# Moving the preparation of the second layer's weights inside the expert units: earlier start steps, a later low-part step, and four block loads spread over steps

## The chip, the cores and the metric

One core of one Trainium2 chip runs the whole program. The metric is the device time of one execution in microseconds (us); lower is better. The kernel before has a median of 1154.63 us over three runs.

## The reference

Attention in chunks of 32 tokens (batch 4, 8 heads, 768 tokens, 16 tokens of left and 8 of right context, 8 memory slots), then a mixture of 8 experts with the best two per token, then a dense layer of three branches:

```python
scores = scale * np.matmul(q_c, k_full.transpose(0, 1, 3, 2))      # attention, chunk by chunk
out[:, :, c_start:c_end] = np.matmul(softmax(scores), v_full)

h = np.maximum(x[mask] @ w1[e], 0.0)                               # experts: 3072 tokens, 512 -> 1024 -> 512
out[mask] += top2_w[mask, k, None] * (h @ w2[e])

h = np.maximum(np.maximum(x @ w1, x @ w2), x @ w3)                 # dense layer: 512 -> 768 -> 512
return h @ w_out
```

## The kernel before

The program is written out in full, one instruction stream for each engine. The order on an engine is the order in which the Python code emits instructions (a manual schedule); an instruction waits only for the data and the buffers that it needs, and what stands behind it on the same engine waits with it.

**Precision.** Each fp32 matrix product is made of three fp32r products: high part by high part, high by low, low by high (`three`, L274). High parts come from a cast on ACT, low parts from a subtraction on DVE.

**Units.** Each expert is worked off in two units (L283 to L286): an even, long one of 512 token slots (four tiles of 128) and an odd, short one of 320 (tiles of 128, 128 and 64); only expert 0 is cut differently. Unit `u` (L785) first makes `h`: 8 steps (`f` = 0 to 7), each of 12 matmuls into one of two PSUM banks, `sc` and `pp`, emptied by ACT (relu, L807) and DVE (low part, L811). Then it makes `y`: 8 steps for each tile, 3 matmuls each, the result copied out at the eighth (`put`, L664, alternately on ACT and DVE) and written to `ys` in DRAM. So a long unit has steps 0 to 39, a short one 0 to 31, and what the unit does on the side is hung on steps: `side[step]` holds tasks that are emitted behind the matmuls of that step.

**On the side.** (1) The next unit's tokens: `unit_turn(u + 1, j)` turns tile j by four PE transposes, casts it on ACT (L193) and forms its low part on DVE (L194). L819 hangs the four turns of a long unit on steps 12, 20, 28 and 36, ahead of what stands there already. A short unit has three tiles, so within a long unit the last turn that does something is the one at step 28. (2) In long units the next weights of the experts (`plan`, 8 parts at steps 0 to 8). (3) **Pieces** of the second layer's weights, which arrive as 64-bit numbers: 24 pieces of 512 KB, for each of `j` = 9, 10, 11, 0, ..., 8 two halves. `planned` (L158) gives each piece a start step `i` and the steps of its five tasks: `one` (ACT square, DVE L231 and L232), `two` (DVE L235 to L237, then the next load into one of three stage buffers), `three` (DVE L241 and four L246), `four` (ACT cast of the high part into the tile `top`, of which there is one buffer, L251) and `five` (DVE low part L255, then two DMAs on SP's queue to `m2s`, L257). Pieces of `j` = 9 to 11 end within `three`. Short units take one piece at step 9; the long units 2, 6, 10 and 14 (odd expert) take two, the long units 4, 8 and 12 (even expert) three. In units 8 and 12 all three pieces go through all five tasks.

**Block loads.** `quad_load(q)` (L756) reads the finished block q of these weights from `m2s` into the weight slots `room[q]`, 1 MB, by a DMA that POOL issues. `ahead` (L766) calls it for q = 0 to 3 at step 2 of unit 14, the last long one, for 4 and 5 at steps 14 and 20 of unit 15. Blocks 0 to 3 go to slots 4 to 7, which hold the second matrix of expert 6, last read in unit 13. Apart from these, POOL issues the gathers of the next unit's tokens (`fetch`, L262), those of unit 15 at step 0 of unit 14. The dense layer (L1009) follows unit 15.

Of the kernel before, what the change touches and what calls it, by code (L numbers as in the profile page):

```python
# [50 lines left out]
def tile_kernel(ctx, tc, qT, kT, mkT, vw, wgn, noise, w1, w2, m2w, out):  # L51
# [103 lines left out]
    turns = [("f64", j, h) for j in (9, 10, 11, *range(9)) for h in range(2)]  # L155
    wparts, plan = list(range(8)), []

    def planned(u):  # L158

        e = u // 2  # L160
        if u == 0:
            return [(8 + k,) for k in range(4)]
        w = [] if u % 2 else [(8 * e + 4 + k, k, k + 1) for k in range(8) if 8 * e + 4 + k < 8 * E]
        at = [9] if u % 2 else [9, 18, 27] if e % 2 == 0 else [9, 22]
        return w + [(turns.pop(0), i, i + 2, i + 4, i + 5, i + 6) for i in at if turns]

    for u in range(2 * E):
        plan.append(planned(u))
        wparts += [x[0] for x in plan[u]]
# [113 lines left out]
    units = []  # L283
# [467 lines left out]
    def fresh(i):  # L751

        t = (wp if i < 8 else big).tile([128, 2, 1024], F32R, name=f"w{i}")
        return t.rearrange("p r n -> p (r n)")

    def quad_load(q):  # L756

        quads[q] = fresh(room[q]).rearrange("p (o k r n) -> p o k r n", o=4, k=2, r=2)
        POOL.dma_start(quads[q], m2s[q, 4:8].rearrange("o p k r n -> p o k r n"))

    def blocks_of(i):

        for q in i:
            quad_load(q)

    def ahead(u, i):  # L766

        if u == len(units) - 2 and i == 2:
            blocks_of(range(4))
        if u == len(units) - 1 and i in (14, 20):  # L770
            quad_load(4 + (i > 14))
        if u == len(units) - 1:
            for k, task, j in ((AF_[0], block_fetch, 0), (AF_[1], block_fetch, 1), (AF_[2], block_mix, 0), (AF_[3], block_mix, 1),
                               (AF_[4], block_turn, 0), (AF_[4], block_fetch, 2), (AF_[5], block_turn, 1), (AF_[5], block_fetch, 3),
                               (AF_[6], block_mix, 2), (AF_[7], block_turn, 2), (AF_[8], block_mix, 3), (AF_[9], block_turn, 3)):
                if k == i:
                    task(0, j)
# [7 lines left out]
    def unit(u):  # L785
# [11 lines left out]
        for f in range(8):  # L797
            p = psum("p")
            for k in range(4):
                three(p[:, 0:n], parts(wtile(8 * e + k), slice(128 * f, 128 * f + 128)),  # L800
                      parts(xT, k, slice(0, n)), k == 0, k == 3)
                if u == 0 and k < 3:
                    tail(f, k)
            if f == 0 and u:
                unit_fetch(u + 1)
            h = hs[f]
            ACT.activation(h[:, 0, 0:n], p[:, 0:n], AF.Relu)  # L807
            whole = n - ns[-1] % 128
            for o, c in ((h[:, 1], slice(0, whole)), (h[:, 0, n - whole:], slice(whole, n))):
                if c.start < n:  # L810
                    DVE.scalar_tensor_tensor(o[:, c], p[:, c], 0.0, h[:, 0, c].bitcast(F32),  # L811
                                             op0=ALU.max, op1=ALU.subtract)
            for task in side[f]:
                task()
            if u == 0:
                tail(f, 3)
            ahead(u, f)
# [3 lines left out]
        for j, m in enumerate(ns):  # L821
            y = psum("y")
            r0 = CAP * e + 128 * (j0 + j)
            for f in range(8):
                w = parts(wtile(8 * e + 4 + f // 2), slice(512 * (f % 2), 512 * (f % 2) + 512))
                if m == 64:
                    for r in range(2):
                        mm(y, hs[f][:, 0, 128 * j:128 * j + 128], w[r], f + r == 0, f + r == 8)
                else:
                    three(y[0:m], parts(hs[f], slice(128 * j, 128 * j + m)), w, f == 0, f == 7)  # L830
                if f == 7 and m == 64:
                    put_sum(ys[r0:r0 + m, :], y)
                elif f == 7:
                    put(ys[r0:r0 + m, :], y, m, last)
                for task in side[8 + 8 * j + f]:
                    task()
                if u == 0:
                    tail(8 + 8 * j + f, 3)
                ahead(u, 8 + 8 * j + f)

    unit(0)
    i = 40
# [211 lines left out]
    with tc.If(most > CAP):  # L1054
# [4 lines left out]
        for k, o in enumerate((dense, tmp)):  # L1059
            w = wt[:, k, :].rearrange("p (t o) -> p t o", o=1).to_broadcast([128, NT, E])  # L1060
# [93 lines left out]
```

## Time and profile before

| | us |
|---|---|
| three runs | 1151.62, 1154.63, 1158.38 |
| median | 1154.63 |
| profiled execution | 1149.49 |
| its span, first to last instruction | 1147.7 |
| PE busy in the span | 1106.3 (96%) |
| DVE busy | 632.7 (55%) |
| ACT busy | 391.6 (34%) |
| POOL busy | 215.9 (19%) |

The profile is one execution. Times of rows are counted from the span's start. "Idle before" in a row is the time for which the engine did nothing ahead of that instruction, and the arrow names what ended it.

### The profile page before, as it was taken

The numbers are of one execution on the slowest core, as the hardware profiler recorded it, in microseconds if no ns is written. First come the engines' busy times: TensorE is split into PE (matmuls) and PEld (weight loads), VectorE is DVE, ScalarE is ACT, GpSimd is POOL, SyncE is SP. The second block draws the span as 40 slices with busy tenths as digits, with TensorE's granted clock in tenths as the row PEclk, the third lists the DMA queues.
The fourth block names the chain that finished last, engine by engine and source line by source line (L and its number), as shares of the span: only waits on it lengthen the run. The fifth ranks groups of instructions, "written<-read, shape, count | busy, mean of one in ns | idle before, by whom it ended". The sixth has DMA issues, their size and how long they took to land. (4 is left out here: it accounts for less than half of the span.)

```text
span 1147.7 us, 17323 instructions
## 1 busy us (share of the span) xinstructions
PE 1106.3 (96%) x6803; PEld 927.2 (81%) x6804; DVE 632.7 (55%) x1258; ACT 391.6 (34%) x680; POOL 215.9 (19%) x237
## 2 busy tenths in 40 slices
PE   7987899999999999999999999999999999999997
PEld 5876778889888888888888887888877878887886
DVE  4586873373474645755646645334765586655221
ACT  5777432232422423424324233222411252113110
POOL 3001010100001001100110020243365525533000
PEclk9999899999999999999999999999999999999999
DMA  8998551261473554755834765375577635668301
GB/s 246 301 291 275 178 167 56 96 214 61 145 247 101 159 172 128 221 149 173 248 97 156 233 192 198 125 230 178 147 220 219 213 120 160 199 182 276 128 1 40
DMA packets 113689, 199.06 MB, mean 173 GB/s; under 512 B 8576, under 2 KB 46592, under 8 KB 113600
## 3 DMA queue, kind: packets, MB, share of 16 engines
q1 hardware_dynamic: 76736, 109.86, 30.4%
q0 software_dynamic: 34272, 78.13, 22.6%
q10 hardware_dynamic: 2592, 9.88, 2.8%
q8 instruction: 56, 0.92, 0.3%
q14 instruction: 33, 0.27, 0.1%
HBM read 151.18 MB, written 46.66 MB: 172 GB/s over the span
## 5 line engine op out<-in xcount | busy, mean ns | idle before, releaser
L93 PE MATMUL sc<-xT,w 128*128 128x512 f32 (+3 forms) x912 | 193.6, 359 | 5.1 <-DVE h L811 3.8
L93 PE MATMUL pp<-xT,w 128*128 128x512 f32 (+3 forms) x912 | 190.5, 356 | 0.0
L93 PEld LDWEIGHTS sc<-xT,w 128*128 128x128 f32 x912 | 157.3, 188 | 29.1 <-ACT h L807 3.1
L93 PEld LDWEIGHTS pp<-xT,w 128*128 128x128 f32 x912 | 157.4, 188 | 19.5 <-DVE h L811 0.2
L264 POOL DMA_INDIRECT g<-xd,tok x56 | 55.1, 984 | 531.3 <-PE idle L271 242.4
L93 PE MATMUL po<-w,h 128*128 128x512 f32 x548 | 135.0, 395 | 0.0
L93 PE MATMUL misc<-w,h 128*128 128x512 f32 x522 | 127.8, 394 | 0.0
L93 PE MATMUL tabp<-w,h 128*128 128x512 f32 x498 | 121.5, 394 | 0.0
L93 PEld LDWEIGHTS po<-w,h 128*128 128x128 f32 x548 | 101.0, 188 | 20.5
L93 PEld LDWEIGHTS misc<-w,h 128*128 128x128 f32 x522 | 96.5, 188 | 19.8
L93 PEld LDWEIGHTS tabp<-w,h 128*128 128x128 f32 x498 | 92.2, 188 | 18.9
L811 DVE SCALAR_TENSOR_TENSOR h<-sc,h 128x256 fp32r<-128x256 f32 (+2 forms) x96 | 39.9, 443 | 91.0 <-ACT h L807 91.0
L213 DVE TENSOR_TENSOR w<-st,w 128x1024 fp32r<-128x1024 f32 x67 | 81.0, 1217 | 11.2 <-ACT w L216 11.0
L811 DVE SCALAR_TENSOR_TENSOR h<-pp,h 128x256 fp32r<-128x256 f32 (+2 forms) x96 | 39.9, 443 | 71.6 <-ACT h L807 71.6
L216 ACT CAST w<-st 128x1024 fp32r<-128x1024 f32 x67 | 70.1, 1046 | 4.4 <-DMA st<-in_w 4.0
L807 ACT ACTIVATE h<-sc 128x512 fp32r<-128x512 f32 (+3 forms) x64 | 33.1, 517 | 111.4 <-PE sc L93 108.7
L264 POOL DMA_INDIRECT g<-ys,rows x48 | 50.6, 1053 | 101.3 <-DMA ys<-y 61.9
L807 ACT ACTIVATE h<-pp 128x512 fp32r<-128x512 f32 (+3 forms) x64 | 33.1, 517 | 80.3 <-PE pp L93 80.2
L93 PE MATMUL po<-v,pt 128*32 128x130 f32 x768 | 30.1, 294 | 17.7 <-ACT pt L383 8.9
L251 ACT CAST top<-val 128x1024 fp32r<-128x1024 f32 x18 | 18.9, 1049 | 80.2 <-DVE val L246 68.3
L194 DVE TENSOR_TENSOR xT<-xp,xT 128x512 fp32r<-128x512 f32 (+1 forms) x35 | 23.3, 666 | 37.8 <-ACT xT L193 37.8
L93 PEld LDWEIGHTS po<-v,pt 128*32 128x32 f32 x768 | 22.3, 115 | 24.2 <-ACT pt L383 12.6
(197 smaller groups left out, 1564.4 us busy)
## 6 DMA issues: line engine op xcount, KB each, us to landing
st<-in_w SPq DMA_DIRECT2D x64, 512.0 KB
w<-m2s POOLq DMA_DIRECT2D x27, 1024.0 KB
st<-in_m2w SPq DMA_DIRECT2D x24, 512.0 KB
ys<-y SPq DMA_DIRECT2D x48, 256.0 KB
m2s<-top SPq DMA_DIRECT2D x18, 512.0 KB
m2s<-val SPq DMA_DIRECT2D x18, 512.0 KB
xT<-m2s POOLq DMA_DIRECT2D x9, 1024.0 KB
w<-m2s POOLq DMA_DIRECT2D x9, 768.0 KB
```

Source lines behind the costliest of these rows:

```text
L93: PE.matmul(o, l, r, start=start, stop=stop)
L194: (eng or POOL).tensor_tensor(lo, src, hi.bitcast(F32), op=ALU.subtract)
L213: (eng or POOL).tensor_tensor(w[:, 1, :], st, w[:, 0, :].bitcast(F32), op=ALU.subtract)
L216: return [n, lambda eng: ACT.copy(w[:, 0, :], st), low]
L251: ACT.copy(hi[0], full)
L264: POOL.indirect_dma_start(out=g[0:n], out_offset=None, in_=src, in_offset=bass.IndirectOffsetOnAxis(ap=idx, axis=0))
L807: ACT.activation(h[:, 0, 0:n], p[:, 0:n], AF.Relu)
L811: DVE.scalar_tensor_tensor(o[:, c], p[:, c], 0.0, h[:, 0, c].bitcast(F32), op0=ALU.max, op1=ALU.subtract)
```

## The change

Pieces start at other steps: in units with an even expert's three pieces at 8, 15 and 22 for 9, 18 and 27, in those with two at 9 and 20 for 9 and 22; in short units the start stays 9. Everywhere task `five` goes from step `i + 6` to `i + 7`, while `four` stays at `i + 5`. The four block loads of unit 14 go from step 2, all at once, to steps 10, 17, 24 and 31.

```diff
-        at = [9] if u % 2 else [9, 18, 27] if e % 2 == 0 else [9, 22]
-        return w + [(turns.pop(0), i, i + 2, i + 4, i + 5, i + 6) for i in at if turns]
+        at = [9] if u % 2 else [8, 15, 22] if e % 2 == 0 else [9, 20]
+        return w + [(turns.pop(0), i, i + 2, i + 4, i + 5, i + 7) for i in at if turns]
@@ def ahead(u, i):
-        if u == len(units) - 2 and i == 2:
-            blocks_of(range(4))
+        if u == len(units) - 2 and i in (10, 17, 24, 31):
+            quad_load((i - 10) // 7)
```

## Rows read from the trace of the kernel before

**Rows 1.** Busy by stretch: units 2 to 11; columns are span, engines, PEclk, DMA, GB/s.
```profile
165.00:601.00 436.00, 433.88 (x2164) 369.35 (x2163) 231.76 (x415) 143.04 (x225) 44.22 (x47) 1.00 0.48 151
```
**Rows 2.** PE's waits, 165 to 760 us: total us, times, longest.
```profile
PE sc L93 <- DVE h L811: 3.8, 3, 1.4
```
**Rows 3.** Timeline of PE, start of unit 13: start, us, line, tile, count, idle before.
```profile
647.14 1.92 PE L93 MATMUL sc<-xT,w 128*128 128x320 f32 x12
648.90 1.92 PE L93 MATMUL pp<-xT,w 128*128 128x320 f32 x12
652.20 1.99 PE L93 MATMUL sc<-xT,w 128*128 128x320 f32 x12 [1.38 <-DVE h L811]
```
**Rows 4.** Timeline of PE, start of unit 9.
```profile
493.18 1.92 PE L93 MATMUL sc<-xT,w 128*128 128x320 f32 x12
...
498.06 1.99 PE L93 MATMUL sc<-xT,w 128*128 128x320 f32 x12 [1.20 <-DVE h L811]
```
**Rows 5.** Timeline of PE, inside unit 14.
```profile
690.76 2.88 PE L93 MATMUL sc<-xT,w 128*128 128x512 f32 x12
693.48 2.88 PE L93 MATMUL pp<-xT,w 128*128 128x512 f32 x12
697.54 3.01 PE L93 MATMUL sc<-xT,w 128*128 128x512 f32 x12 [1.17 <-DVE h L811]
```
**Rows 6.** Timeline of ACT, end of unit 12 and start of unit 13.
```profile
641.33 1.05 ACT L251 CAST top<-val 128x1024 fp32r<-128x1024 f32 x1 [5.72 <-DMA m2s<-top]
...
642.85 0.36 ACT L193 CAST xT<-xp 128x256 fp32r<-128x256 f32 x1
...
648.68 1.05 ACT L251 CAST top<-val 128x1024 fp32r<-128x1024 f32 x1 [4.99 <-DVE val L246]
649.64 0.43 ACT L807 ACTIVATE h<-sc 128x320 fp32r<-128x320 f32 x1
```
**Rows 7.** Timeline of DVE, the same stretch.
```profile
642.41 1.23 DVE L255 TENSOR_TENSOR val<-val,top 128x1024 fp32r<-128x1024 f32 x1 [1.21 <-ACT top L251]
643.55 0.42 DVE L231 TENSOR_SCALAR val<-st 128x512 int32<-128x512 int32 x1
...
644.61 0.42 DVE L194 TENSOR_TENSOR xT<-xp,xT 128x256 fp32r<-128x256 f32 x1
644.95 0.68 DVE L235 SCALAR_TENSOR_TENSOR val<-sq,val 128x512 f32<-128x512 f32 x1
...
646.85 0.69 DVE L241 TENSOR_TENSOR val<-val,sq 128x512 f32<-128x512 f32 x1
...
650.91 0.68 DVE L670 COPY y<-misc 128x512 f32<-128x512 f32 x1
```
**Rows 8.** Timeline of SP's queue, unit 12: the first piece's high part goes out.
```profile
634.95 0.43 SPq L257 DMA_DIRECT2D m2s<-top  x1
```
**Rows 9.** Timeline of DVE, end of unit 8: the second piece's low part.
```profile
488.27 1.23 DVE L255 TENSOR_TENSOR val<-val,top 128x1024 fp32r<-128x1024 f32 x1 [1.04 <-ACT top L251]
```
**Rows 10.** Timeline of DVE and PE, end of unit 10 (two pieces).
```profile
566.32 0.42 DVE L194 TENSOR_TENSOR xT<-idle,xT 128x256 fp32r<-128x256 f32 x1 [1.43 <-ACT xT L193]
...
570.88 1.92 PE L93 MATMUL sc<-xT,w 128*128 128x320 f32 x12
```
**Rows 11.** Timeline of SP's queue and ACT, unit 14: a load and its cast.
```profile
688.10 0.38 SPq L186 DMA_DIRECT2D st<-in_w  x1
...
695.22 1.05 ACT L216 CAST w<-st 128x1024 fp32r<-128x1024 f32 x1 [3.60 <-DMA st<-in_w]
```
**Rows 12.** Timeline of POOL: the four block loads of unit 14.
```profile
676.85 2.52 POOL L759 DMA_DIRECT2D w<-m2s  x3 [0.34 <-DMA m2s<-top]
680.00 0.74 POOL L759 DMA_DIRECT2D w<-m2s  x1 [0.63 <-DVE xT L194]
```
**Rows 13.** Timeline of PE: the first matmul of unit 14.
```profile
679.33 0.40 PE L93 MATMUL sc<-xT,w 128*128 128x512 f32 x1
```
**Rows 14.** Busy by stretch with the granted clock (PEclk, third number from the end).
```profile
120.00:130.00 10.00, 7.35 (x84) 6.28 (x75) 7.35 (x25) 4.39 (x8) 0.00 (x0) 0.83 0.66 206
```

## The prediction

> **What bounds the kernel now.** I read the busy table by stretch first, then PE's waits, then PE's timeline around each wait, then the timelines of the engine named there. In the experts' stage PE is the bound and nearly full: busy 433.88 of 436.00 us over units 2 to 11 [rows 1]. The list of PE's waits for this stage is short: one kind of any size, the first products of a unit waiting for DVE to empty the bank `sc`, 3.8 us in three waits [rows 2]. They stand at the third group of unit 13, the third group of unit 9, and within unit 14 [rows 3 to 5]. All that this change can take out of PE's path lies in these three. From group starts the loss is a little more than the idle shown, since a wait also stretches the work beside it: unit 13, 652.20 - 648.90 = 3.30 where the step before took 1.76, so 1.54 us; unit 9, 498.06 - 493.18 = 4.88 for two groups of 1.76, so 1.36; unit 14, 697.54 - 693.48 = 4.06 where the step before took 2.72, so 1.34 [rows 3 to 5]. Sum 4.24 us of 1154.63, 0.37%.
>
> What is behind them differs. At the start of units 9 and 13 the third piece of the unit before runs late. In unit 12 its task `four` is cast on ACT at 648.68, after PE has begun unit 13 at 647.14, and ACT's relu comes only at 649.64 [rows 3, 6]; DVE then still has the low part and an output copy (650.91) ahead of the relu's low part [rows 7]. In unit 14 a weight load issued at 688.10 is cast at 695.22, ACT having waited 3.60 us for its landing [rows 11], while the four block loads of 1 MB, issued from 676.85 to 680.00, were on their way [rows 12].
>
> **The pieces in short units, and in long units with two.** In short units only `five` moves, from step 15 to 16; nothing but the output copy of step 15 is near, and that is ahead of it before and after. Cost nothing. In units 2, 6, 10 and 14 the second piece starts at 20 instead of 22. Its `one` stays behind the turn of step 20, `four` (27, then 25) stays ahead of the turn of step 28, so ACT's order is the same; on DVE `five` (28, then 27) now goes ahead of that turn's low part instead of behind it, 1.23 us by [rows 7]. In unit 10 that low part ran at 566.32 and PE began the next unit at 570.88 [rows 10]: 566.32 + 1.23 + 0.42 = 567.97, so 2.9 us of cover are left. Cost nothing; if the cover were gone, at most 1.2 us in each of four units.
>
> **Units 8 and 12.** Here the order changes, and I follow unit 12. The first piece keeps its order on both engines (its `one` goes one step earlier with nothing in between, and waits for its load anyway). The second and third start 3 and 5 steps earlier, but steps are places in a queue, not times. The queue has two real limits. First, `top` is one buffer: ACT's cast of piece 2 waited 5.72 us, until 641.33, for the DMA of piece 1's high part, which SP had issued at 634.95 [rows 6, 8]. That DMA depends on piece 1, which does not move, so the second cast stays at 641.33 and piece 2's `five` at 642.41 [rows 7]. Second, DVE's work from there: `one` of piece 3 begins at 643.55, 1.06 us to 644.61; `two` 1.90 us (644.95 to 646.85); `three` up to the cast 1.83 us (646.85 to 648.68); and now also the output copy of step 23, 0.68 us, which fell before 642.41 until now, since `five` of piece 2 was at step 24 and goes to 22 [rows 6, 7]. So piece 3's cast can start at 643.55 + 1.06 + 0.68 + 1.90 + 1.83 = 649.02. That is no sooner than the 648.68 of before.
>
> What changes is who stands behind it. Before, `four` of piece 3 was at step 32, behind the turn of step 28, and the turn's cast ran at 642.85 [rows 6]. Now `four` is at 22 + 5 = 27, one step ahead of that turn. ACT takes its instructions in order, so the turn's cast waits for piece 3's: 649.02 + 0.96 (648.68 to 649.64, one cast to the next) = 649.98, plus 0.36 = 650.34; DVE's low part 0.42 more = 650.76 [rows 6, 7]. This tile is the last 64 tokens of unit 13, and every matmul of its first group reads them. PE wants them at 647.14 [rows 3]. It can do one product with high parts alone (1.76 / 12 = 0.15), so it loses 650.76 - 647.14 - 0.15 = 3.5 us. The late work of before is then over while PE does its first two groups: the old loss of 1.54 goes. In unit 8, piece 2's `five` is at 488.27 and PE's start at 493.18, 154.14 and 153.96 us ahead of unit 12's [rows 4, 7, 9]; the same sum gives 3.3 us where 1.36 goes. Together 6.8 - 2.9 = 3.9 us more. Unit 4 has three pieces too, but the first two end within `three` and never use `top`; I put its cost at nothing.
>
> The price has a lower end: if nothing held piece 2's cast, DVE's idle 1.21 us ahead of 642.41 [rows 7] would be saved in each, leaving 3.9 - 2.4 = 1.5 us. Its upper end is a clock matter, below.
>
> **`five` two steps behind the copy.** DVE's idle of 1.21 and 1.04 us ahead of `five` [rows 7, 9] looks like what this is for. In the long stretch it is worth nothing here: what DVE did not wait for in `five` it waits for elsewhere, as the cast itself is late.
>
> **The four block loads.** They are emitted at steps 10, 17, 24 and 31, but POOL does not keep step with PE. With step 2 they were issued from 676.85, before PE's first matmul of unit 14 at 679.33 [rows 12, 13], as each slot came free. Ahead of them on POOL's queue are the gathers of unit 15, behind them those of the dense layer, before and after; SP's queue is not touched. POOL has nothing else in this unit, and slots 4 to 7 and blocks 0 to 3 are ready as they were. So POOL's stream is the same instructions in the same order with the same conditions: they go at the same times, the late cast of [rows 11] stays, and so do unit 14's 1.34 us. Cost and gain nothing; bounds -1.3 (the wait goes) and 0.
>
> **Sum.** 0 + 3.9 + 0 + 0 = 3.9 us. The profiled execution took 1149.49 us (span 1147.7), 5.1 under the median; none of the terms depends on that, so 1149.49 becomes 1153.4 and the median 1154.63 becomes 1158.5, 0.34% more. A measurement of this kernel can tell about 0.5% (5.8 us) from no change, so this counts as the same.
>
> **The rivals.** (a) Slower beyond that: the clock. Stretches of before in which PE stood idle more are followed by a lower clock: from 120 to 130 us PE was busy 7.35 of 10 us, and the granted clock averaged 0.83, that is, 0.17 x 10 = 1.7 us lost to the 1.2 GHz level [rows 14]. Two idle times of 3.3 and 3.5 us in a stage that had none over 1.5 may do this once or twice: 1160.2 or 1161.9. It decides the sign as measured if it happens at both places. For it: the idle time is more than doubled. Against it: the waits of before [rows 3 to 5] did not do it, and PE was full until then.
>
> (b) The landing of piece 1's high part is quicker. The chain rests on 634.95 to 641.33, 6.4 us for 512 KB. By the rows the time is then 1154.6 + 1.5 = 1156.1. The Trainium skill, page "DMA: Bandwidth & Descriptors", section "Anatomy of one DMA", fits about 2.0 us plus the bytes over 436 GB/s, an estimate of 3.2 us here, and by it the cast would not be held at all; the measured 6.4 us, on queues shared with loads and outputs, speaks against it, and the sum goes by the row.
>
> (c) It gains as its steps suggest: the third piece is over before PE reaches the next unit, and the losses at units 9 and 13 go, 1154.6 - 2.9 = 1151.7. For that its cast must start by 647.14 - 0.96 - 0.36 - 0.42 = 645.4, and I count 649.0. Only a piece 1 that ends 3.6 us sooner does it.
>
> (d) The change does with the block loads what it says: they are spread, the load of [rows 11] lands in time, and 1.3 us come off: 1157.2. Against it [rows 12, 13].
>
> **How the numbers follow.** Forecast with the clock held 0.45; (a) 0.24; (b) 0.12; (c) 0.11; (d) 0.06; nothing of this seen 0.02. The likeliest is 1158.5. The range takes in (a), (b) and (d), and the spread of the runs of before, a few us: 1153.0 to 1163.0; it leaves out (c) and the tails. Faster by over 0.5% (under 1148.9) is not in any case and comes from spread alone, 0.03. Slower by over 0.5% (over 1160.4): most of (a), and a few hundredths of spread on the forecast, 0.25. The same: 0.72.
>
> **What would show it.** In the profile after: at the starts of units 9 and 13 PE's first group waits some 3 us for the turn (ACT L193 or DVE L194), and the old waits at the third group are gone; ACT's cast of 128x256 comes just behind the cast `top` of piece 3; the block loads still go just before unit 14's first matmul; the 1.2 us wait within unit 14 is there. I am wrong if the turn's cast is ahead of the third `top` cast, if that cast starts well before PE's next unit, or if the block loads stand apart in time.

## The result and the profile after

The changed kernel takes 1157.12 us (median of 22 runs), the kernel before 1151.51 us in as many; the ratio is 1.0054, 95% interval 1.0042 to 1.0066, that is 6.2 us more (4.8 to 7.6; the medians differ by 5.6). The forecast was 3.9 us more with a range of 1153.0 to 1163.0 us. The profiled execution took 1158.85 us, its span 1157.0.

Where the time came from can be read to a tenth, since two units of one expert take the same time in every profile when nothing disturbs them: from the first matmul of unit 10 to that of unit 12 it is 76.2 to 76.3 us in all profiles of this study. The table has the three stretches in which something does, each worked out from the starts of first matmuls in PE's timeline.

| us | units 8 and 9 | units 12 and 13 | unit 14 to the dense layer | sum |
|---|---|---|---|---|
| before | 77.70 | 77.89 | 78.16 | 233.75 |
| after | 80.51 | 81.51 | 78.47 | 240.49 |

So 6.7 us of the difference between the two profiles lie in these three stretches, 2.81 and 3.62 of them in the first two. The spans differ by 9.3; the other 2.6 us were lost ahead of unit 1's first matmul (at 177.80 us before, 180.49 after), where the two programs are the same (last section).

PE's list of waits from 170 to 765 us of the changed kernel (total, times, longest) is to be held against [rows 2]:

```profile
PE sc L93 <- ACT xT L193: 5.4, 2, 3.2
PE sc L93 <- DVE h L811: 1.5, 1, 1.5
```

Two of the three waits for DVE's low part of `h` are gone (the one left is in unit 14), and two longer ones for ACT's cast of the next unit's tokens have come. PE's timeline at the starts of units 9 and 13, which answers to [rows 3, 4]:

```profile
493.66 2.20 PE L93 MATMUL tabp<-w,h 128*128 128x512 f32 x9
498.06 2.86 PE L93 MATMUL sc<-xT,w 128*128 128x320 f32 x12 [2.19 <-ACT xT L193]
500.71 2.98 PE L93 MATMUL pp<-xT,w 128*128 128x320 f32 x12
503.53 1.92 PE L93 MATMUL sc<-xT,w 128*128 128x320 f32 x12
...
649.78 2.88 PE L93 MATMUL misc<-w,h 128*128 128x512 f32 x12
655.83 3.48 PE L93 MATMUL sc<-xT,w 128*128 128x320 f32 x12 [3.16 <-ACT xT L193]
659.10 2.35 PE L93 MATMUL pp<-xT,w 128*128 128x320 f32 x12
661.29 1.92 PE L93 MATMUL sc<-xT,w 128*128 128x320 f32 x12
```

The wait is now at the first group, not the third. And the groups behind it are slow: from 498.06 to 500.71 and to 503.53 they take 2.65 and 2.82 us, from 655.83 to 659.10 and 661.29 3.27 and 2.19, where a group of this size takes 1.76. The table by stretch says why; the third number from the end is the granted clock:

```profile
495.00:510.00 15.00, 12.77 (x73) 12.05 (x72) 6.44 (x18) 3.99 (x8) 0.00 (x0) 0.89 0.48 157
650.00:665.00 15.00, 11.79 (x62) 10.78 (x61) 8.04 (x19) 3.12 (x6) 0.00 (x0) 0.89 0.63 207
```

In each stretch some 0.11 x 15 = 1.7 us were lost to the lower level of 1.2 GHz. Before, the clock was 1.00 around both places:

```profile
490.00:505.00 15.00, 13.80 (x86) 13.01 (x85) 8.71 (x22) 3.13 (x6) 0.00 (x0) 1.00 0.72 214
647.00:662.00 15.00, 13.62 (x93) 13.35 (x92) 6.78 (x20) 4.01 (x8) 0.00 (x0) 1.00 0.46 149
```

ACT's and DVE's timelines at the end of unit 12 show who held the tokens, against [rows 6, 7]:

```profile
646.83 1.06 ACT L251 CAST top<-val 128x1024 fp32r<-128x1024 f32 x1 [5.86 <-DMA m2s<-top]
...
654.46 1.04 ACT L251 CAST top<-val 128x1024 fp32r<-128x1024 f32 x1 [6.01 <-DVE val L246]
655.41 0.37 ACT L193 CAST xT<-xp 128x256 fp32r<-128x256 f32 x1
```
```profile
647.92 1.23 DVE L255 TENSOR_TENSOR val<-val,top 128x1024 fp32r<-128x1024 f32 x1 [1.76 <-ACT top L251]
649.06 0.42 DVE L231 TENSOR_SCALAR val<-st 128x512 int32<-128x512 int32 x1
...
650.13 0.68 DVE L670 COPY y<-tabp 128x512 f32<-128x512 f32 x1
...
655.81 0.42 DVE L194 TENSOR_TENSOR xT<-xp,xT 128x256 fp32r<-128x256 f32 x1 [1.43 <-ACT xT L193]
```

The third piece's cast is at 654.46, the turn's cast directly behind it, its low part at 655.81; the output copy stands between `one` and `two` of the piece. POOL's block loads, against [rows 12, 13]: unit 14's first matmul is at 688.34 here, and three of the four loads were issued from 685.86, the last at 689.01:

```profile
685.86 2.52 POOL L759 DMA_DIRECT2D w<-m2s  x3 [0.33 <-DMA m2s<-top]
689.01 0.74 POOL L759 DMA_DIRECT2D w<-m2s  x1 [0.63 <-DVE xT L194]
```

### The profile page after: what moved, and what is told of

The parts are those of the page before. It is cut to its first block, busy times and chain, and to the rows that moved or that the text cites. A ratio compares the mean times of both kernels' runs of the same rounds, so it can differ in the third digit from the quotient of the medians.

```text
span 1157.0 us, 17333 instructions
## 1 busy us (share of the span) xinstructions
PE 1111.9 (96%) x6803; PEld 932.7 (81%) x6804; DVE 633.3 (55%) x1258; ACT 392.1 (34%) x680; POOL 216.0 (19%) x237
```

## The experiments

The theory: the change's cost is in units 8 and 12 alone; the last turn of these units is caught behind the late third piece; the longer wait of PE lets the clock fall, and this costs as much again; the block loads do not move. The rivals: the loads have a share; the pieces are too dense wherever the turn stands; the clock is no part of the cost. Stretches are given as in the table above (sum before: 233.75).

**The block loads alone.**

```diff
-        if u == len(units) - 2 and i == 2:
-            blocks_of(range(4))
+        if u == len(units) - 2 and i in (10, 17, 24, 31):
+            quad_load((i - 10) // 7)
```

> The kernel before with the block loads alone moved to steps 10, 17, 24 and 31 of unit 14. My theory: POOL runs ahead of PE and has nothing else in this unit, so its instructions are the same in the same order: all four loads are issued before or at unit 14's first matmul, the wait of 1.2 us inside unit 14 stays, ratio 1.000. Rival (the loads are really spread): loads some 5 to 9 us apart, that wait gone, 1.3 us less, ratio 0.9988.

Ratio 1.0005 (0.9985 to 1.0025), stretches 77.53, 78.03 and 78.25. POOL's timeline:

```profile
677.42 2.52 POOL L759 DMA_DIRECT2D w<-m2s  x3 [0.34 <-DMA m2s<-top]
680.58 0.74 POOL L759 DMA_DIRECT2D w<-m2s  x1 [0.63 <-DVE xT L194]
```

These are the issues of [rows 12] with 0.6 us on the clock of the span: a step in the program that is 8 to 29 steps later moved nothing. So this part of the change is without effect.

**The pieces alone** (the other half of the diff).

> The changed kernel with the block loads back at step 2. My theory: all of the change's cost is in the pieces, so this is the changed kernel again, ratio 1.005 (1.004 to 1.007), PE's waits at the starts of units 9 and 13 about 2.4 and 3.4 us, each followed by a granted clock of 0.5. Rival (the loads' place has a share in it): clearly nearer to 1.000 or above 1.007.

Ratio 1.0073 (1.0050 to 1.0096), stretches 81.09, 81.61 and 78.19: the changed kernel again as far as the intervals tell, which overlap. The ratio itself, of six runs, lies a little above the 1.007 at which the rival began. Its profile has 0.4 us more in the three stretches, at unit 9, where PE waited 2.77 us instead of 2.19; in unit 8 the second piece's cast came 6.1 us after SP issued the first piece's high part (484.62 to 490.74), in the changed kernel 5.5 (483.52 to 489.06). The clock fell at both places here too (0.89). That the loads have no share is told better by the run with them alone.

**The third piece's cast behind the turn.**

```diff
-        return w + [(turns.pop(0), i, i + 2, i + 4, i + 5, i + 7) for i in at if turns]
+        return w + [(turns.pop(0), i, i + 2, i + 4, i + 6, i + 7) for i in at if turns]
```

> The changed kernel with one number changed: task four at step i + 6 instead of i + 5, so that the third piece's cast in units 8 and 12 (step 28) stands behind the turn of step 28 on ACT and no longer ahead of it. My theory (the turn's cast caught behind a late cast): the waits at the first group of units 9 and 13 go, the late low part holds the third group as in the kernel before (1.2 to 1.6 us each), the clock stays at 1.00 there, ratio 1.000 (0.999 to 1.001). Rival (the earlier steps crowd DVE, whatever the cast's place): the waits stay at 2 to 3.5 us, ratio 1.003 to 1.005.

Here the theory fell short. Ratio 1.0054 (1.0031 to 1.0077), stretches 78.23, 79.89 and 77.88. ACT casts the turn early, and PE still waits, 1.70 us at unit 9 and 1.84 at unit 13, now for DVE (timelines of ACT, DVE and PE, end of unit 12):

```profile
646.56 0.35 ACT L193 CAST xT<-xp 128x256 fp32r<-128x256 f32 x1
```
```profile
651.56 1.02 DVE L246 TENSOR_TENSOR val<-val 128x128 f32<-128x128 f32 x4
652.50 0.42 DVE L194 TENSOR_TENSOR xT<-xp,xT 128x256 fp32r<-128x256 f32 x1
```
```profile
650.83 0.30 PE L93 MATMUL sc<-xT,w 128*128 128x320 f32 x1
652.97 2.49 PE L93 MATMUL sc<-xT,w 128*128 128x320 f32 x11 [1.84 <-DVE xT L194]
```

PE does its one product with high parts and stops: `three` of the third piece, at step 26, stands ahead of the turn of step 28 on DVE as well. The cast on ACT was the longer of two holds, not the only one. This edit also puts the cast of the first piece in some units behind an output copy; no wait of PE shows that.

**The same again**, because the time lay above the 2.2 us more that the profile's stretches give.

> The same kernel as e3_cast_behind_turn, since its time (1.0031 to 1.0077) was above what its one profile showed in units 8 to 15 (2.2 us over the kernel before, with one clock of 0.5). By the profile: PE waits for DVE's low part of the turn 1.8 us at each first group, and if the clock falls after both in most executions, 0.6 + 2 x 1.7 = 4.0 us, ratio 1.0035; if it falls after one of them, 1.002. Rival (the change has a cost outside these units that no wait shows): 1.005 or more with the stages outside units 8 to 15 longer than in the kernel before.

Ratio 1.0022 (1.0003 to 1.0040), stretches 77.99, 80.03 and 78.14, 2.4 us more in sum, with a clock of 0.89 from 650 to 665 us and 1.00 from 495 to 510. This time run and profile agree. Whether the first seven runs were really slower is open: the two intervals overlap from 1.0031 to 1.0040, and a fall of the clock at unit 9 as well, which neither profile shows, would add 1.7 us.

**The third piece at 24.**

```diff
-        at = [9] if u % 2 else [8, 15, 22] if e % 2 == 0 else [9, 20]
+        at = [9] if u % 2 else [8, 15, 24] if e % 2 == 0 else [9, 20]
```

> The changed kernel with the third piece's start at 24 instead of 22: tasks one and two (24, 26) stay ahead of the turn of step 28, three (28) and four (29) fall behind it, on DVE and on ACT. My theory (what counts is the work that stands ahead of the turn on both engines): the turn's low part comes some 1.8 us sooner than with a third piece at 22 whose cast alone is behind the turn, so PE waits 0.5 us or less for it at the first groups of units 9 and 13, the waits at the third groups are 1.2 to 1.8 us, no clock of 0.5 there; units 8 to 15 as long as in the kernel before to within 1 us, ratio 1.0005 (0.999 to 1.002). Rival (any start ahead of 27 costs): waits of over 1.5 us at the first group, ratio 1.003 or more.

Ratio 1.0017 (1.0001 to 1.0033), stretches 78.33, 78.99 and 78.35, 1.9 us more. At unit 13:

```profile
649.95 1.88 PE L93 MATMUL sc<-xT,w 128*128 128x320 f32 x11 [0.69 <-DVE xT L194]
651.66 1.92 PE L93 MATMUL pp<-xT,w 128*128 128x320 f32 x12
655.14 1.99 PE L93 MATMUL sc<-xT,w 128*128 128x320 f32 x12 [1.56 <-DVE h L811]
```

With `three` and `four` behind the turn, 0.69 us of the wait for the turn are left (0.5 or less was expected) and the old wait at the third group is back; the clock does not fall. The sum was above the 1 us expected, since both waits are there at once.

**The turn ahead of the whole third piece.**

```diff
         for i, a in enumerate(spread(tasks, 8 * len(ns))):
+            i -= 7 * (u in (8, 12) and i == 20)
             side[8 + i] = a + side[8 + i]
```

> The changed kernel with the third turn of units 8 and 12 hung on step 21 instead of 28, so that its transposes, cast and low part stand ahead of all of the third piece on every engine. My theory (the turn is caught behind the third piece on ACT and on DVE): the waits of units 9 and 13 at the first group go, those at the third group come back with 1.2 to 1.6 us each, no clock of 0.5 there, ratio 1.000 (0.999 to 1.001). Rival (the three pieces as such are too dense, wherever the turn stands): waits of 2 us or more stay and the ratio stays at 1.003 or more.

Ratio 1.0005 (0.9988 to 1.0023), stretches 77.74, 77.67 and 77.96, with all three pieces as dense as in the changed kernel. PE's waits are those of before:

```profile
PE sc L93 <- DVE h L811: 3.4, 3, 1.3
```

So it is the turn's place behind the piece, on both engines, and not the density of the pieces.

**The clock.** Two kernels fill PE's wait with matmuls of zeros that nobody reads; what is computed stays as it was.

```diff
+        if u in (9, 13):
+            spin(po_b[:, 1], 11 if u == 9 else 15)
         for f in range(8):
             p = psum("p")
```

> The changed kernel with matmuls of zeros that nobody reads, 128x512 bf16 into an unused bank, 11 ahead of unit 9's first group and 15 ahead of unit 13's, to fill the time in which PE waits. My theory (the clock's fall after these waits costs about as much as the longer waits): the turn's cast and low part come at the same times, the granted clock stays 1.00 over units 9 and 13, 2 x 1.7 = 3.4 us come back, ratio 1.0054 - 0.0030 = 1.0025. Rival (the waits alone are the cost, the clock only looks bad): ratio stays at 1.005, or gets worse by the added matmuls.

Ratio 1.0054 (1.0036 to 1.0073), stretches 79.42, 83.81 and 77.98. At unit 9 it did what it should; at unit 13 it did not. The filler's bank belongs to a tile of two banks, and an output copy was still reading the other one; that copy stood on ACT behind the same late cast:

```profile
653.21 5.09 PE L93 MATMUL po<-warm,ones 128*128 128x512 bf16 x15 [2.45 <-ACT y L668]
```

So the filler came after the wait, on top of it, and the clock fell there too (0.89 from 650 to 665 us). The second kernel takes the bank `idle`.

```diff
+        if u in (9, 13):
+            spin(idle, 11 if u == 9 else 15)
```

> The changed kernel with the same 11 and 15 matmuls of zeros ahead of the first groups of units 9 and 13, now into the bank idle, which no late output copy holds, so that they run from the moment PE would wait. My theory: no granted clock of 0.5 in units 9 and 13, the waits for the turn as in the changed kernel (first true product at the same place after the unit before), so the time falls by the clock's share alone, 2 x 1.7 = 3.4 us under the changed kernel: ratio to the kernel before 1.0035 (1.002 to 1.005). Rival (the clock is no part of the cost): 1.0055 to 1.007, as the changed kernel.

Ratio 1.0024 (1.0004 to 1.0043), stretches 79.41, 79.52 and 77.99. PE's timeline at unit 13, and the two stretches with the clock:

```profile
649.94 2.97 PE L93 MATMUL idle<-warm,ones 128*128 128x512 bf16 x13
652.56 2.11 PE L93 MATMUL sc<-xT,w 128*128 128x320 f32 x12
```
```profile
495.00:510.00 15.00, 14.79 (x96) 13.60 (x95) 5.64 (x17) 4.86 (x10) 0.00 (x0) 1.00 0.43 137
650.00:665.00 15.00, 15.00 (x97) 13.55 (x97) 5.67 (x16) 4.42 (x9) 0.00 (x0) 1.00 0.42 139
```

PE does useless work while it would wait, and the kernel is faster by it: the first two stretches fall by 80.51 - 79.41 = 1.10 and 81.51 - 79.52 = 1.99, 3.1 us together. An earlier start is not what did it: counted from the unit before, the first group begins 0.4 us later at unit 9 and 0.2 us earlier at unit 13 (there the tokens came 1.2 us sooner than in the changed kernel, and the filler held PE). From its first matmul to that of the next unit, unit 9 takes 30.99 us where it took 32.52, and unit 13 takes 30.76 where it took 32.51. So 1.5 and up to 1.8 us came back with the clock, and the rival that the clock is no part of the cost falls.

**The loads really spread.**

```diff
+    def quad_load(q, eng=POOL):
...
-        POOL.dma_start(quads[q], m2s[q, 4:8].rearrange("o p k r n -> p o k r n"))
+        eng.dma_start(quads[q] if eng is POOL else quads[q].bitcast(F32), m2s[q, 4:8].rearrange("o p k r n -> p o k r n"))
...
-        if u == len(units) - 2 and i == 2:
-            blocks_of(range(4))
+        if u == len(units) - 2 and i in (10, 17, 24, 31):
+            quad_load((i - 10) // 7, SP)
```

> The kernel before with the four block loads issued by SP's queue at steps 10, 17, 24 and 31 of unit 14, among the loads and outputs of these steps, so that they cannot run ahead. My theory of unit 14's wait (the load of the first steps lands late under the four block loads): issues lie some 5 us apart from about 698 us on, the load issued at the second group lands in 3.5 us instead of 7.1, the wait of 1.2 us goes, ratio 0.9988 (0.998 to 1.000). Rival (what is spread out collides with the last outputs and the gathers behind them): the wait goes but comes back at the first block, ratio 1.000 or more.

SP's timeline has the loads among the work of their steps; the first line is the load of [rows 11]. Its cast is in ACT's timeline:

```profile
686.42 0.38 SPq L186 DMA_DIRECT2D st<-in_w  x1
...
695.01 0.39 SPq L759 DMA_DIRECT2D w<-m2s  x1
...
710.21 1.41 SPq L759 DMA_DIRECT2D w<-m2s  x1
...
714.75 1.14 SPq L759 DMA_DIRECT2D w<-m2s  x1
...
723.91 0.39 SPq L759 DMA_DIRECT2D w<-m2s  x1
```
```profile
690.00 1.05 ACT L216 CAST w<-st 128x1024 fp32r<-128x1024 f32 x1
```

The load is cast 3.6 us after its issue, where it was 7.1 before. The third stretch falls from 78.16 to 76.69, and unit 14's wait is gone from PE's list; the dense layer has no new one, though it takes 0.3 us longer (390.5 for 390.2). So the cause of that wait, four loads at once over the load of [rows 11], is shown, as far as the queue that issues them, which this edit changes with the time, has no share in it. The ratio, 0.9994 (0.9976 to 1.0013), holds both 0.9988 and 1.000, so in time alone the gain of 1.5 us is not told.

**What the steps were after.** The loads as in the last kernel, the pieces as in the kernel before, and the tasks `four` and `five` of the third piece in the next unit:

```diff
-        return w + [(turns.pop(0), i, i + 2, i + 4, i + 5, i + 6) for i in at if turns]
+        return w + [(turns.pop(0), i, i + 2, i + 4, *((41, 43) if i == 27 else (i + 5, i + 6))) for i in at if turns]
...
-            side = [[] for _ in range(steps)]
+            side = [later.pop(i, []) for i in range(steps)]
...
-                    side[t].append(partial(task_of, part, now, i))
+                    (side[t] if t < steps else later.setdefault(t - steps, [])).append(partial(task_of, part, now, i))
```

> The kernel before with the block loads from SP as in e7_loads_from_sp and, of the third piece of units 4, 8 and 12, the tasks four and five carried into the next unit, at its steps 1 and 3; all else as before. My theory: the turn is ahead of the piece's cast as before, and the late cast and low part stand behind the first relus, so the waits of units 9, 13 and 14 all go: 1.36 + 1.54 + 1.34 = 4.2 us less, ratio 0.9963 (0.995 to 0.998). Rival (DVE and ACT are as late at the start of units 9 and 13, whatever the piece's rest does): those two waits stay, 0.9985 or more.

Ratio 0.9962 (0.9945 to 0.9980), 1144.91 us beside 1149.41 for the kernel before in the same comparison; stretches 76.27, 76.27 and 76.71, so units 8 to 13 are undisturbed. PE's list of waits for this stage has nothing over 0.2 us at a time left, and ACT's timeline at unit 13 shows the late cast where it holds nobody:

```profile
PE sc L93 <- issue: 0.9, 4, 0.2
PE sc L93 <- DVE xT L194: 0.5, 2, 0.2
```
```profile
647.39 0.44 ACT L809 ACTIVATE h<-pp 128x320 fp32r<-128x320 f32 x1 [1.32 <-PE pp L93]
647.73 1.04 ACT L251 CAST top<-val 128x1024 fp32r<-128x1024 f32 x1
649.15 0.44 ACT L809 ACTIVATE h<-sc 128x320 fp32r<-128x320 f32 x1 [0.39 <-PE sc L93]
```

This kernel is faster than both.

## Why the prediction was right, and where it was not

**What bounds the kernel, and how much there was to win:** right. The three waits of [rows 3 to 5] were worth what was counted, 4.24 us: with all three gone the kernel takes 4.4 us less (1149.41 x 0.0038).

**Short units and long units with two pieces:** right, nothing. Units 10 and 11 take 76.27 us before and 76.25 after.

**Units 8 and 12:** right in the mechanism. For unit 13 the forecast put the third piece's cast 1.88 us and the end of the turn's low part 3.62 us behind PE's wanted start (649.02 and 650.76 beside 647.14). In the changed kernel PE was ready at 649.78 + 12 x 0.227 = 652.50 (a matmul here takes 2.72 / 12); the cast is at 654.46, 1.96 us behind, and the low part ends at 655.81 + 0.42 = 656.23, 3.7 us behind. PE began its group 3.3 us late.

For unit 9 the forecast of 3.3 us was too much: PE was ready at 493.66 + 9 x 0.227 = 495.70 and began at 498.06, 2.4 us late; by the forecast's own measure, the end of the turn's low part (498.46) less one product, the loss is 2.6. The term that was off is the landing of the first piece's high part, rival (b) in small: in unit 8 of the changed kernel the second piece's cast came 5.5 us after that DMA's issue, where the chain rested on 6.4, and the second piece's low part, 493.18 - 488.27 = 4.9 us ahead of PE's wanted start before [rows 4, 9], was at 490.15 (DVE's timeline), 5.55 us ahead. In unit 12 the same landing took 6.5 us (640.32 to 646.83), and the cast waited 5.86 us for it.

The estimate of 3.2 us that (b) took from the Trainium skill's page "DMA: Bandwidth & Descriptors" (section "Anatomy of one DMA") was far off in both units. That section gives its fit for DMAs that POOL issues; this one is on SP's queue.

One sentence of that step was incomplete. The turn was said to be held by ACT's order; the run with the cast behind the turn shows that DVE's order holds it too; PE's waits are 0.5 and 1.3 us shorter there. The sum took the later of the two, so the number stood.

**The block loads:** right, as the run with them alone shows. The loads are spread in the program and not in time. Rival (d) had the price of a real spread about right: 1.3 us foretold, 1.5 us in the stretch of the run that spreads them.

**The clock:** the step that was mis-weighed. It was rival (a), with a chance of 0.24 beside 0.45 for a held clock, and in the profile it came at both places, with the 1.7 us each that the prediction had read from [rows 14]. What had been put against it, that the waits of [rows 3 to 5] did not do it, was no evidence for waits of twice that length. The forecast's 3.9 and 3.4 for the clock make 7.3; the shorter loss at unit 9 takes off 0.7, which gives 6.6, where the two stretches show 6.4 and the runs 6.2. So what happened is not the likeliest case but (a) at both places, for which 1161.9 had been given. That 1157.12 lies so near to 1158.5 is luck in part: the kernel before came out at 1151.51, 3.1 us under the 1154.63 that the forecast was added to, while by its medians the change cost 1.7 us more than the 3.9 forecast. The measured 0.54% also lies just over the 0.5% up to which the prediction called the two kernels the same; with 22 runs of each, the interval (0.42 to 0.66%) tells it from no change.

**`five` two steps behind the copy:** the forecast was no cost and no gain, and no run has this edit alone. By the code, the order of instructions on every engine would then be that of the kernel before.

## What to carry to other kernels

A step in the program is a place in a queue, not a time: moving a task to a lower step makes it little earlier when a buffer or a full engine holds it (the third piece's cast, five steps lower, came 0.4 us sooner in unit 8 and 0.4 us later in unit 12, counted from the time PE was ready), but it puts it ahead of whatever stood in between, and on each engine the task issues to, so list what is overtaken and by when that is needed. An engine that runs ahead, as POOL does here, was not moved by its step at all; the transfers were spread only when an engine that is tied to the work of that step issued them. And price a longer wait of PE with the clock behind it: here 2.4 and 3.3 us of waiting cost 1.7 us each on top.

## What the runs showed of the hardware that was not expected

After the waits of the changed kernel the granted clock fell at both places, with 2.2 and 3.2 us of idle PE. With the cast behind the turn it fell at unit 13 after 1.8 us in the first profile and 2.0 in the second, and not at unit 9 after 1.7 and 1.5; at the waits of 1.0 to 1.6 us at the units 9 and 13 of the other kernels it did not fall. Filling the wait with matmuls that nobody reads made the kernel faster.

The time to the first matmul of unit 1, up to which all kernels here are the same, was 175.7 to 182.1 us in their profiles, with a granted clock over the first 165 us between 0.94 and 0.97, as in these two (the kernel before is in the first line, the kernel with the turn ahead in the second):

```profile
0.00:165.00 165.00, 138.33 (x2180) 117.54 (x2182) 114.62 (x341) 106.54 (x168) 17.53 (x43) 0.97 0.82 246
```
```profile
0.00:165.00 165.00, 138.26 (x2160) 118.05 (x2162) 111.56 (x331) 106.70 (x168) 16.79 (x42) 0.94 0.80 241
```

So a stretch ahead of the change varies by as much as the whole change costs. The stretches of the table above are of one profile each, but they leave this part out.
